# Sorting matrix of a block-sorted attention: two batches normalized on 128 partitions with column sums by TensorE, the other two later, and another load order

## The chip, the cores and the metric

The kernel runs on one core of one Trainium2 chip. The metric is the device time of one execution in microseconds (us); lower is better. The kernel before has three timed runs, with a median of 218.76 us (218.69 to 218.97). A further execution was profiled.

## The reference, cut to what matters

An attention over 4 batches, 8 heads, 768 positions and head size 64, whose keys and values are first mixed by blocks. P is an 8x8 matrix per head and batch, made from `sort_net` by five rounds of exp, row normalization and column normalization. The attention's output, 3072 tokens of width 512, goes through a feed-forward layer with a squared relu.

```
P = sort_net                                  # (4, 8, 8, 8)
for _ in range(5):
    P = exp(P - max(P, axis=-1))
    P = P / (sum(P, axis=-1) + 1e-09)
    P = P / (sum(P, axis=-2) + 1e-09)
k_sorted = einsum('bhij,bhjcd->bhicd', P, k_b)   # 8 blocks of 96 positions
v_sorted = einsum('bhij,bhjcd->bhicd', P, v_b)
attn = softmax(q_b @ k_sorted^T / 8)             # block by block, 96 x 96
x = (attn @ v_sorted) with heads side by side    # (3072, 512)
out = relu(x @ w_in) ** 2 @ w_out                # 512 -> 2048 -> 512
```

## The kernel before

Inputs are loaded by DMAs that POOL issues (function `dma`, line 319; the issue itself is L322) and that cast fp32 to bf16. Batch 0 is loaded as q in two halves of 64 partitions, then k and v by head pairs (k0, v0, k1, ... v3), then w_in in four quarters. w_out and batch 1 are loaded after the last of the three builds of w_all that POOL makes; batches 2 and 3 are loaded when attention of the batch before has come far enough (`load_late`).

P of all 32 heads lies on 32 partitions, 64 numbers each (`p_sb`). In each of five rounds ACT takes the exp (L432) and DVE normalizes rows, then columns (`sink_norm`, L400 to L402). Then DVE turns P (`p_turn`, L443), eight small matmuls spread it over the partitions (`p_spread`, L450), and `build_w` (L462) multiplies the spread P by a mask of the diagonal: w_all, the right side of the matmuls that mix k and v. For batch 0, w_all is built in pieces: heads 0 and 1, and 2 and 3, first half of the output blocks, by DVE; then, by POOL, heads 4 to 7 first half, heads 0 to 3 second half, heads 4 to 7 second half. The copy of the spread P, `pt` (L1075), is the source for all but the first. For batches 1 (second half of heads), 2 and 3, k and v are mixed by another form of P, `w_t` (`build_wt`, L487 and L494).

One unit of attention is a pair of heads. Its stages, with the letters that the order lists use, are K and V (`s_sort`, L588: mix k or v of the pair, then a copy), S (`s_sc`, L667 or L657: scores, then exp on ACT), T (`s_vt`, L723: transpose v, then a copy), A (`s_av`, L873: probabilities times v, then `norm` on DVE, L885 and L886) and X (`s_xt`, L928 or a DMA transpose: turn the result into xT). The first half of batch 0 (384 tokens) is computed first; its second half has K as `s_sort2` (L624). N is the mixing by w_t (`s_nat`, L759), Z the turning of k and q by DMA.

The feed-forward layer takes 384 tokens at a time: 64 "up" matmuls (L997), relu on ACT (L1005), square on DVE (L1008), 48 "down" matmuls (L1027), a copy and a DMA to the output. The first such unit needs xT of all four pairs of the first half of batch 0. Single matmuls of it, F0 to F7, are put ahead of that (`f_piece`, L955).

The order of the work on each engine is worked out before the program is written: every piece is an `Op` with an engine, a cost, and what it depends on, and `Plan.run` (L136) hands the pieces out in simulated time. On PE there are two lists, taken from the front only: attention and feed-forward. The attention piece goes if it could start earlier, or if its due number (a count of feed-forward pieces) is reached. On the other engines the piece that can start first goes; of equal ones, the one added first. Each engine then runs its pieces in that order. The string `FIRST` (L53) is the attention order of the first half of batch 0: a letter for the stage, a digit for the pair, a capital for a copy by ACT and a small letter for DVE, a quote mark for the other buffer in PSUM. `DUES` (L21) holds the due numbers of all later stages. Where PE would idle before its first feed-forward unit, `fill` (L418) puts matmuls on ones.

The softmax here doesn't subtract the row's maximum and nothing guards it: scores larger than these inputs give would overflow.

## Time and profile before

| What | Value |
|---|---|
| median of three runs | 218.76 us |
| the profiled execution | 218.47 us |
| its span, first to last instruction | 216.70 us |
| PE busy in the span | 210.8 us (97%) |
| first build of w_all begins | 11.88 us |
| last transposes of the first half of batch 0 begin | 20.90 us |
| last "down" matmul ends, by the chain of waits | 213.87 us |
| granted TensorE clock | 1.00 |

The profile is that of one execution. A row of the timeline gives start, busy time, engine, line, operation, what is written and read, and in brackets the idle time before it and what ended that. The chain of waits follows the work that ended last back from its end: each row is a start, a length and what was running. A busy PE is a PE with a matmul in it, filler matmuls included.

### The profile page before, as it was taken

The numbers are of one execution on the slowest core, as the hardware profiler recorded it, in microseconds if no ns is written. First come the engines' busy times: TensorE is split into PE (matmuls) and PEld (weight loads), VectorE is DVE, ScalarE is ACT, GpSimd is POOL, SyncE is SP. The second block draws the span as 40 slices with busy tenths as digits, with TensorE's granted clock in tenths as the row PEclk, the third lists the DMA queues.
The fourth block names the chain that finished last, engine by engine and source line by source line (L and its number), as shares of the span: only waits on it lengthen the run. The fifth ranks groups of instructions, "written<-read, shape, count | busy, mean of one in ns | idle before, by whom it ended". The sixth has DMA issues, their size and how long they took to land.

```text
span 216.7 us, 4912 instructions
## 1 busy us (share of the span) xinstructions
PE 210.8 (97%) x1942; PEld 120.1 (55%) x1958; DVE 109.9 (51%) x310; ACT 120.6 (56%) x246; POOL 30.5 (14%) x55
## 2 busy tenths in 40 slices
PE   8989999999999999999999999999999999999994
PEld 2566666446566565346675455446666465456543
DVE  6778748218784446506886055327676155005400
ACT  4665795237955277417884277238765276137521
POOL 7995223200000600000000420000000000000000
PEclk9999999999999999999999999999999999999999
DMA  5999999999983699299982599559996310120012
GB/s 66 196 202 207 207 207 206 184 222 274 201 176 98 123 192 215 51 182 205 242 158 78 125 193 213 109 142 127 257 188 135 91 51 0 48 82 18 0 48 97
DMA packets 47831, 31.51 MB, mean 145 GB/s; under 512 B 27264, under 2 KB 42880, under 8 KB 47808
## 3 DMA queue, kind: packets, MB, share of 16 engines
q0 software_dynamic: 12736, 13.63, 38.7%
q1 hardware_dynamic: 35072, 17.56, 36.5%
q8 instruction: 15, 0.25, 0.4%
q14 instruction: 8, 0.07, 0.1%
HBM read 29.70 MB, written 8.72 MB: 177 GB/s over the span
## 4 chain that ended last, share of the span: by engine, by line
PE 90%; DVE 5%; ACT 2%; issue 1%; DMA 1%; DVEq 0%
PE hp L997 38%; PE op L1027 36%; PE p L873 4%; PE p L657 3%; PE p L759 2%; PE op L1055 2%; PE p L667 1%; PE vbp L723 1%; DVE p_sb L402 1%; PE p L624 1%; DMA p_sb<-in_sort_net_dram 1%; ACT h L1005 1%; PE xtp L928 1%; DVE cs L400 1%; ACT p_sb L432 1%
## 5 line engine op out<-in xcount | busy, mean ns | idle before, releaser
L997 PE MATMUL hp<-xT,w_in_bf 128*128 128x384 bf16 x506 | 87.8, 326 | 0.0
L1027 PE MATMUL op<-w_out_bf,h 128*128 128x512 bf16 x352 | 83.5, 379 | 0.8
L1008 DVE TENSOR_TENSOR h<-h 128x384 bf16<-128x384 bf16 x128 | 43.9, 355 | 57.4 <-ACT h L1005 57.1
L1005 ACT ACTIVATE h<-hp 128x384 bf16<-128x384 f32 x128 | 62.0, 494 | 18.1 <-PE hp L997 15.6
L997 PEld LDWEIGHTS <-w_in_bf 128*128 128x128 bf16 x506 | 47.7, 98 | 31.3 <-issue 0.9
L1027 PEld LDWEIGHTS <-h 128*128 128x128 bf16 x368 | 34.4, 98 | 37.0 <-issue 1.0
L248 ACT COPY ob<-op 128x512 f32<-128x512 f32 (+2 forms) x25 | 14.2, 569 | 51.5 <-PE op L1027 49.1
L886 DVE TENSOR_TENSOR ao<-p,rec 96x512 bf16<-96x512 f32 x32 | 22.0, 687 | 1.1
L697 ACT ACTIVATE et<-p 96x384 bf16<-96x384 f32 x40 | 16.8, 486 | 8.0 <-PE p L657 7.7
L873 PEld LDWEIGHTS <-et 96*128 96x128 bf16 x256 | 11.6, 97 | 5.0 <-issue 0.7
L885 DVE RECIPROCAL rec<-p 96x8 f32<-96x8 f32 x32 | 6.4, 201 | 10.6 <-PE p L873 8.8
L1139 POOL COPY held<-xT 1x3 bf16<-1x3 bf16 (+1 forms) x2 | 0.4, 184 | 78.6 <-DMA xT<-ao 78.6
L418 PE MATMUL p<-ones 128*128 128x512 bf16 (+1 forms) x30 | 9.8, 449 | 1.1 <-DVE ones L269 1.1
L657 PEld LDWEIGHTS <-kx 128*128 128x128 bf16 x80 | 8.5, 144 | 2.3 <-issue 0.2
L873 PE MATMUL p<-vblk,et 96*128 96x65 bf16 x192 | 9.5, 193 | 0.0
L657 PE MATMUL p<-qz,kx 128*128 128x192 bf16 x80 | 9.0, 246 | 0.0
L250 DVE CAST kn<-p 128x768 bf16<-128x768 f32 x5 | 4.8, 957 | 8.3 <-PE p L759 8.1
L250 DVE CAST vn<-p 128x768 bf16<-128x768 f32 x6 | 5.7, 956 | 5.8 <-PE p L759 4.4
L322 POOL DMA_DIRECT2D kb<-in_k_dram x10 | 6.4, 637 | 4.4 <-DMA w_in_bf<-in_moe_w_in_dram 2.0
L322 POOL DMA_DIRECT2D qb<-in_q_dram x8 | 6.1, 769 | 5.8 <-DVE h L1008 3.3
L322 POOL DMA_DIRECT2D vb<-in_v_dram x10 | 6.2, 621 | 3.3 <-DMA w_in_bf<-in_moe_w_in_dram 3.3
L248 ACT CAST kn<-p 128x768 bf16<-128x768 f32 x5 | 4.0, 803 | 4.3 <-PE p L759 4.3
(84 smaller groups left out, 125.2 us busy)
## 6 DMA issues: line engine op xcount, KB each, us to landing
out_dram<-ob SPq DMA_DIRECT2D x23, 256.0 KB, 2.2
qb<-in_q_dram POOLq DMA_DIRECT2D x8, 384.0 KB, 11.3
v_way<-vn SPq DMA_DIRECT2D x6, 396.0 KB, 5.5
vblk<-v_way SPq DMA_DIRECT2D x6, 396.0 KB, 4.2
vb<-in_v_dram POOLq DMA_DIRECT2D x6, 384.0 KB, 12.0
kb<-in_k_dram POOLq DMA_DIRECT2D x6, 384.0 KB, 10.7
w_in_bf<-in_moe_w_in_dram POOLq DMA_DIRECT2D x4, 512.0 KB, 11.8
w_out_bf<-in_moe_w_out_dram POOLq DMA_DIRECT2D x4, 512.0 KB, 18.1
```

The lines of the kernel that those rows point to most:

```text
L248: nc.scalar.copy(out=out, in_=in_)
L250: nc.vector.tensor_copy(out=out, in_=in_)
L322: nc.gpsimd.dma_start(out=dst, in_=src)
L418: nc.tensor.matmul(out=p2[slot][:, 0, 0:128 * r].rearrange("p (r x) -> p r x", r=r), lhsT=ones, rhs=ones[:, None, :].to_broadcast([128, r, ...
L657: nc.tensor.matmul(out=scp[:, n // 2, 2 * BLK * (n % 2):2 * BLK * (n % 2 + 1)], lhsT=kx_r[u.kx][:, i::NB], rhs=qz_r[u.qz][:, :, :, C0 * i: ...
L697: nc.scalar.activation(out=et.rearrange("p h x -> p (h x)")[:, HS * h:HS * (h + 1)] .rearrange("p (m c a) -> p m c a", c=C0, a=NA), in_=st ...
L873: nc.tensor.matmul(out=oup[:, h, 66 * n:66 * n + D + 1], lhsT=(et_r[u.et[hf]].rearrange("p h x -> p (h x)") [:, BLK * (2 * n + h):BLK * (2 ...
L886: nc.vector.tensor_tensor(out=u.ao[:, n0:n0 + NQ, :, :].rearrange("p n e d -> p e n d"), in0=ov[:, :, :, 0:D], in1=rec[:, :, :, None].to_b ...
L997: nc.tensor.matmul(out=t["hp", nt][:, 0:HS], lhsT=w_in_bf[:, kc, 128 * nt:128 * (nt + 1)], rhs=xT[:, kc, t0:t0 + HS], start=(kc == 0), sto ...
L1005: nc.scalar.activation(out=t["h1", nt], in_=t["hp", nt][:, 0:HS], func=AF.Relu)
L1008: nc.vector.tensor_tensor(out=t["h2"][:, nt, :], in0=t["h1", nt], in1=t["h1", nt], op=ALU.mult)
L1027: nc.tensor.matmul(out=t["op", mt], lhsT=t["h2"][:, nt, 128 * mt:128 * (mt + 1)], rhs=w_out_bf[:, nt, :], start=(nt == 0), stop=(nt == NT ...
```

## The change

For batches 0 and 1, P lies on 128 partitions, one row of a matrix each (`pj`, 8 numbers). The exp gives the row sums as well (`accum_out`). Column sums are one fp32 matmul per round with a block-diagonal matrix of ones, `blk`, that DVE sets and POOL cuts out (`make_blk`). The last round writes P repeated 16 times, `pb`, and a single matmul with the identity spreads it. Fillers are planned ahead of the column-sum matmuls too.

P of batches 2 and 3 keeps the old form, and is made later (`late_p`), once the last pair of batch 0's second half is done; its `sel` is written by POOL and no longer by ACT. `build_wt` is called twice, for the second half of batch 1's heads and for batches 2 and 3.

Loads of batch 0 come in the order of `LOADS`; w_in comes in five pieces, the first two of two column tiles each (128 columns), and each "up" matmul waits for its own piece. The transposes of the second half of q move from ahead of P's spread into `FIRST` as Q0 to Q3, and those of the first half move in between the rounds of P. `FIRST` and `DUES` are new.

```diff
-FIRST = ("K0' v0 K1 v1 S0 t0 S1 t1' A0 k2' V2 A1 K3 S2 t2' v3 S3 x0 A2 T3' x1 A3 X2' F0 F3 F1 "
-         "x3 F4 F6 F7")
+LOADS = "q0 k0 v0 q1 k1 v1 k2 v2 k3 v3 w0"
+FIRST = ("P0 v0 Q3 k0 K1 S0 v1' T0' q2 S1 q1 K2' A0 V2 t1' S2 T2' A1 x0' K3 V3' A2 S3 t3 F0 x1' A3 "
+         "F3 x2 Q0 F1 x3 F4 F6 F7")
...
-    (2, "N"): (75.5, 70.5),
-    (2, "V"): (63.0, 88.5),
+    (2, "N"): (66.0, 82.5),
+    (2, "V"): (72.5, 88.5),
...
-    (3, "N"): (130.0, 137.5),
-    (3, "V"): (117.0, 140.5),
+    (3, "N"): (137.0, 139.0),
+    (3, "V"): (117.0, 142.0),
...
+    (2, "P"): (22.0,),
+    (2, "W"): (51.0,),
...
+    NF = 2 * H
+    pj = const.tile([128, NB], FP32)
+    nc.sync.dma_start(out=pj, in_=sort_net.rearrange("b h i j -> (b h i) j")[0:128, :])
     p_sb = const.tile([NH, NB, NB], FP32)
     nc.sync.dma_start(out=p_sb, in_=sort_net.rearrange("b h i j -> (b h) i j"))
...
+    blk = const.tile([128, 128], FP32)
+    nc.vector.memset(blk, 1.0)
...
     def load_w_in(g):
-        f = slice(d_ff // 4 * g, d_ff // 4 * (g + 1))
+        t0, t1 = ((0, 2), (2, 4), (4, 8), (8, 12), (12, 16))[g]
+        f = slice(128 * t0, 128 * t1)
...
-    load(0, 0, 0, H, slice(0, 64))
-    load(0, 0, 0, H, slice(64, 128))
-    id_op = plan.add("POOL", 0.4, lambda e: make_identity(nc, ident, nomemset=True))
+    def make_blk(e):
+
+        view = blk.rearrange("p (g x) -> p g x", x=NB)
+        for base, step, mult in ((0, -NB, 1), (NB - 1, NB, -1)):
+            nc.gpsimd.affine_select(
+                out=view, in_=view, compare_op=ALU.is_ge, fill=0.0, base=base,
+                pattern=[[step, 128 // NB], [0, NB]], channel_multiplier=mult)
+
+    load_next(1)
+    blk_op = plan.add("POOL", 0.65, make_blk)
+    id_op = plan.add("POOL", 0.35, lambda e: make_identity(nc, ident, nomemset=True))
+    load_next(4)
...
     plan.add("POOL", 1.5, make_mask, [id_op])
-    for g in range(HP):
-        load(0, 1, 2 * g, 2)
-        load(0, 2, 2 * g, 2)
-    load_w_in(0)
-    for g in range(1, 4):
+    load_next(len(loads))
+    for g in range(1, 5):
         load_w_in(g)
...
+    def by_rows(e):
+        nc.vector.reciprocal(out=rr, in_=rr)
+        nc.vector.tensor_tensor(out=pj, in0=pj, in1=rr.to_broadcast([128, NB]), op=ALU.mult)
+
+    def add_rows(e):
+        tiles["sums"] = ps1.tile([128, NB], FP32, tag="p1", name="sums")
+        nc.tensor.matmul(out=tiles["sums"], lhsT=blk, rhs=pj, start=True, stop=True)
+
+    def by_columns(e, last):
+        nc.vector.reciprocal(out=cr, in_=tiles["sums"])
+        if last:
+            nc.vector.tensor_tensor(
+                out=pb, in0=pj[:, :, None].to_broadcast([128, NB, C0]),
+                in1=cr[:, :, None].to_broadcast([128, NB, C0]), op=ALU.mult)
+        else:
+            nc.vector.tensor_tensor(out=pj, in0=pj, in1=cr, op=ALU.mult)
...
     for it in range(5):
-        step = plan.add("ACT", 0.26, lambda e: nc.scalar.activation(
-            out=p_sb, in_=p_sb, func=AF.Exp), [step])
+        step = plan.add("ACT", 0.25, lambda e: nc.scalar.activation(
+            out=pj, in_=pj, func=AF.Exp, accum_out=rr), [step])
         exps.append(step)
-        step = plan.add("DVE", 0.66, lambda e: sink_norm(e, 0), [step])
-        step = plan.add("DVE", 0.69, lambda e, it=it: sink_norm(e, 1, it == 4), [step])
+        step = plan.add("DVE", 0.36, by_rows, [step])
+        slot, old = r1.take()
+        step = plan.add("PE", 0.2, add_rows, [step, blk_op] + old)
+        fast.append(step)
+        r1.use(slot, step)
+        step = plan.add("DVE", 0.5 if it == 4 else 0.38, lambda e, it=it: by_columns(e, it == 4), [step])
+        r1.use(slot, step)
...
+    def late_p(due):
+
+        gate = x_done[0, HP - 1, 1]
+        picked = plan.add("POOL", 1.5, make_sel, [gate])
+        step = gate
+        for it in range(5):
+            step = plan.add("ACT", 0.26, lambda e: nc.scalar.activation(
+                out=p_sb, in_=p_sb, func=AF.Exp), [step])
+            for axis in range(2):
+                step = plan.add("DVE", 0.22, lambda e, axis=axis: late_sums(e, axis), [step])
+                step = plan.add("DVE", 0.2, lambda e, axis=axis: late_inverse(e, axis), [step])
+                step = plan.add("DVE", 0.22, lambda e, axis=axis, last=it == 4 and axis == 1:
+                                late_scale(e, axis, last), [step])
+        step = plan.add("DVE", 0.23, p_turn, [step])
...
+    def spread_first():
+        sf, old = rf.take()
+        pe = plan.add("PE", 0.1, p_spread, [last, id_op] + old)
+        spreads.append(pe)
+        w0 = build_w(0, 2, None, pe, 0, NQ)
+        cp = spread[0] = plan.add("ACT", 0.28, lambda e: nc.scalar.copy(out=pt, in_=tiles["pt_ps"]), [pe])
+        rf.use(sf, w0, cp)
+        build_w(2, 2, pt, cp, 0, NQ)
+        builds.extend(build_w(h0, 4, pt, cp, i0, NQ, "POOL") for h0, i0 in ((4, 0), (0, NQ), (4, NQ)))
...
+                if op in fast:
+                    fill(op.gap - 0.2, slot, 0.45 if op.begin < 4.5 else 0.24)
+                else:
+                    fill(op.gap - (0.5 if op in spreads else 0.05), slot)
```

## The prediction, made before the change was run

> **What bounds the kernel now.** I first read the page's shares and slices. PE is the engine to watch.
>
> ```profile
> PE 210.8 (97%) x1942; PEld 120.1 (55%) x1958; DVE 109.9 (51%) x310; ACT 120.6 (56%) x246; POOL 30.5 (14%) x55
> PE   8989999999999999999999999999999999999994
> DMA  5999999999983699299982599559996310120012
> ```
>
> A busy PE includes filler matmuls (the rows of L418), so I went on to the chain of waits, from 20 us.
>
> ```profile
> 20.15 0.70 DVE ao L886
> 20.85 0.05 issue
> 20.90 0.34 PE xtp L928 x4
> 21.24 0.49 PE hp L955 x3
> 21.73 0.88 PE p L624 x48
> 22.61 0.16 PE wtp L487 x4
> 22.77 1.73 PE hp L997 x10
> ...
> 85.87 0.50 ACT h L1005
> 86.37 0.02 issue
> 86.39 0.37 DVE h L1008
> ```
>
> From 20.90 us, the transposes that end head pair 3 of the first half (x3 in FIRST), the chain is PE work to 213.87 us, but for three places like the one at 85.87 (one each at 182.09 and 202.85) and some 0.05 us gaps. So there are two ways to change the time: move the 20.90, or add PE work behind it. What moves the 20.90? The timeline of POOL:
>
> ```profile
> 9.75 0.72 POOL L322 DMA_DIRECT2D vb<-in_v_dram  x1
> 10.46 2.30 POOL L322 DMA_DIRECT2D w_in_bf<-in_moe_w_in_dram  x3
> 12.98 0.74 POOL L322 DMA_DIRECT2D w_in_bf<-in_moe_w_in_dram  x1 [0.21 <-issue]
> 13.74 1.84 POOL L462 TENSOR_TENSOR w_all<-mask,pt 128x256 bf16<-128x256 bf16 x3
> 15.53 3.03 POOL L322 DMA_DIRECT2D w_out_bf<-in_moe_w_out_dram  x4
> 19.78 0.55 POOL L322 DMA_DIRECT2D vb<-in_v_dram  x1 [1.22 <-DMA w_in_bf<-in_moe_w_in_dram]
> ```
>
> POOL issues all loads of batch 0 and of w_in, and only then builds w_all for heads 4 to 7. The builds had their input since 12.57 us (pt cast, 12.20 + 0.37) and began at 13.74, when the last w_in load was issued. Issue-to-landing times of single loads give a second fact: v1, the 6th load, landed at 6.90 + 5.8 = 12.70 and the 14th was issued at 12.98; w_in 0, the 11th, landed at 10.46 + 9.0 = 19.46 and the 19th was issued at 19.78. An issue that waits begins some 0.3 us after the landing of the load eight before it.
>
> ```profile
> L322 POOL DMA_DIRECT2D kb<-in_k_dram x1: 716/716/716, 7.6 to 7.6; - x1
> DMA to landing us min/median/max: 6.8/6.8/6.8
> ```
>
> This is k2 (for heads 4 and 5), the 7th load: landed at 7.62 + 6.8 = 14.4. By the same sum v2 landed at 15.0, k3 at 16.0, v3 at 16.95.
>
> **What the Trainium skill says.** "TensorE: Matmul & The Clock Gate", section "Part 1: The HAM clock gate", gives about 427 ns per 512-column matmul on a cold array, about 216 warm. The trace agrees: fillers load their weights every 0.43 us up to 4.9 us; later 512-column matmuls take 0.216. The same page, section "Architectural detail", says that ScalarE, VectorE and GpSimd take their queues strictly in order, and that TensorE reorders nothing but weight loads; the POOL rows above agree (the builds wait 1.1 us behind loads). "FP8 and Floating Point Precision", section "TensorE Precision Notes", says a true fp32 product is four passes; no row of before shows one.
>
> **Part 1: the P chain.** Before, an iteration takes 4.07 - 2.31 = 1.76 us from exp to exp: one exp 0.26 and six DVE operations 0.21 + 0.19 + 0.21 + 0.25 + 0.19 + 0.21, with gaps. The first w_all build begins at 11.88. After, on 128 partitions: exp with row sums 0.25 (below: 0.19, fixed cost; above: 0.45 if the sum is a second instruction); two DVE operations 0.38; the fp32 matmul 0.35 (below 0.24, the wait from p_ij to the first spread matmul; above 0.6, four weight loads of 0.1 and the wait of one); reciprocal from PSUM and product 0.40; four changes of engine 0.2. That is 1.58, and 0.9 us less over five. The turn by DVE (0.23) and seven of eight spread matmuls go too: 0.9 and 0.5 for these turn 11.88 into about 10.5 (9.6 with all lower ends, 12.7 with all upper ones). One more cost is possible: fillers stand ahead of the sum matmuls on PE. The gap before the second is about 1.2 us and is filled at 0.24 each, with the array cold until about 5 us, so four of them take 1.7 and push the chain by 0.5, perhaps again in the third.
>
> **Part 2: what waits instead.** The new load order moves k0, v0 ahead of the second half of q; the bytes ahead of k2, v2, k3, v3 are the same and DMA is full from 4 us, so these land when they did. But POOL's list ahead of the builds grows by make_blk (two selects at the 0.32 of the ident row) and by one load, as w_in comes in five pieces. Sum: first load at 1.26, done 2.02; blk 2.7; ident 3.1; four loads at 0.72 to 6.0; mask 1.61 (3.84 to 5.45 before) to 7.6; six loads at 0.73 to 12.0; three pieces of w_in at 0.77 to 14.3. The 15th load needs the 7th, k2, landed: 14.4 + 0.3 = 14.7, issued by 15.45. First build 1.84 / 3 = 0.61: done at **16.1** (15.7 if nothing is limited to eight). Before it was 14.35, and K2 ran at 15.05 behind A0. P being ready 1.4 us earlier doesn't help: the planner gives POOL the loads first, as their start is never later than that of the builds.
>
> In the new FIRST, K2' stands before A0, V2, t1', S2, T2', A1, x0', K3. PE takes them in order, so all of these wait for 16.1, though A0 could run near 14.3 to 15 (before, it ran 14.69 - 11.88 = 2.8 after the first build; 10.5 + 2.8, and about 1 for the q and v1 pieces now ahead of it). From K2' on, with the durations of before: sort to copy 0.42, copy 0.48 on ACT; scores to exp 0.38, exp 0.80; transposes to copy 0.44, copy 0.42 on DVE or 0.58 on ACT; A to norm 0.5, norm 0.93. Times from K2': A0 0.2, t1' 0.76; norm 0 to 1.6 and the t1 copy behind it on DVE to 2.0, so A1 at 2.1; x0', K3 at 2.6, V3' at 2.8; ACT copies K3 to 3.5 and V3 to 4.0; S3 3.6, its exp to 4.8; t3 at 4.1, but its copy stands on DVE behind norm 1, x0 and norm 2, to 5.2; A3 5.3, norm to 6.65; x3 at 6.7. Before, it was 20.90 - 15.05 = 5.85 with A0, t1 and the q copies already out of the way. So x3 falls at 22.8; with 15.7 and DVE's order better than mine, 22.0. I take **22.5**, which is 1.6 later than 20.90 (1.1 to 2.0).
>
> **Part 3: late P.** Its spread is eight matmuls (0.26, the weight loads of that row before) and a second wtp group (0.16): 0.42 more PE work in the saturated part, up to 0.6 with changes of tiling. Its 30 DVE operations and five exps are 5 x 1.76 = 8.8 us from about 36 us on. DVE is busy 2.77 of 5 us from 35 to 40 and 2.63 of 10 from 40 to 50, so they fit; a square of L1008 may stand behind one waiting operation, and the down matmuls behind that square: 0 to 0.3, I take 0.1. If that cover were gone the price is one iteration, 1.8. sel moves to POOL, idle there from 39 to 71 us: nothing. The second p_sb load goes on SP behind the first, one issue of 0.40, with SP idle to 29 us: nothing.
>
> **Part 4: q and the due numbers.** Four groups of q transposes, hidden in the chain before, now stand in FIRST; three of them lie in PE's wait for K2', one in the norm of pair 3: nothing, 0.25 each on PE if that cover is gone. w0 with two tiles lands near 18.2 instead of 19.46, ahead of F0's turn: nothing. The due numbers reorder attention pieces of the same sizes; they can fill or lay open a stall like that at 85.87, of which 0.4 to 0.5 is real (two op matmuls run within the 0.9): -0.4 to +0.4, I take 0.
>
> **Sum.** 1.6 + 0.42 + 0.1 = +2.1 us. The profiled execution took 218.47 us (span 216.70 and 1.77 around it): 218.47 + 2.1 = **220.6**. The median of the runs is 218.76, 0.29 above the profiled one, so the forecast stands rather low against it.
>
> **Rivals.**
> A, builds not late (POOL gets to them before its last w_in issues, or faster): then v3's landing decides. 16.95 plus a bare chain (sort, copy, transpose, copy, A, norm: 3.5) puts x3 at 20.45, 0.45 earlier, and the 0.5 of part 3 takes it back: 218.5. For it: PE and ACT have room; against: the POOL rows. Chance 0.18.
> B, the gain comes through: P's 1.4 us earlier moves x3 by as much, 218.47 - 1.4 + 0.5 = 217.5; or A with the stalls filled, 218.1. One mechanism decides, whether anything stands between P and x3: it needs v3 well before 16.95 and the builds before 14. Against: the full DMA row, and 20.45 as the earliest x3. For: P's chain is all that PE waits for until 11.88. Chance 0.20, faster.
> C, worse: the cold fillers and four-pass matmuls put P at 12 to 12.7, the q pieces and S1 end after 16.1 and push A0 by 0.5 to 1; or late P holds the squares. 221.5. Chance 0.12.
> The forecast has 0.50.
>
> **How the numbers follow.** Against 218.76, a change of under 0.2% (0.44 us) is about what measurement can't tell from none: 218.3 to 219.2. Forecast and C are slower, 0.62; A is the same, 0.18; B is faster, 0.20. The range from 218.0 to 221.9 leaves out most of B and the worst of C. The likeliest case alone, slower, spans 219.7 to 221.3.
>
> **What would show it.** Right: POOL's w_all row begins near 15.5; PE waits on POOL for K2 at about 16; xtp of pair 3 begins after 22; the chain is solid PE from there, with a late-spread row and two wtp rows. Wrong: the sorts of heads 4 and 5 start by 14.6, or xtp begins before 21. Part 1 is wrong if the first w_all build is later than 11.6.

## The result, and the profile after the change

| | before | after |
|---|---|---|
| median of four runs | 218.87 us | 225.28 us (224.57 to 225.71) |
| ratio to before, 95% interval | | 1.0289 (1.0261 to 1.0318) |
| profiled execution / its span | 218.47 / 216.70 us | 225.71 / 224.0 us |
| first build of w_all begins | 11.88 | 12.35 |
| K2 begins on PE | 15.05 | 16.57 |
| last transposes of the first half begin | 20.90 | 24.50 |
| last down matmul ends | 213.87 | 220.77 |

The kernel became slower, by 6.4 us and not by the 2.1 of the forecast; 225.28 is above the range. In the profiled executions the difference is 225.71 - 218.47 = 7.24 us. It splits at the mark that the prediction used: 3.60 up to the last transposes of the first half, 3.30 from there to the last down matmul ((220.77 - 24.50) - (213.87 - 20.90)), and 0.40 - 0.06 in what lies behind and around the span.

Runs of one kernel that holds the change differ by up to 4.4 us, so most experiments below are read by places in their profiles (each a single run) rather than by their medians; a run over 1.5% above the fastest of its kernel counts as slow and is left out of medians and ratios, and as the profiles of e1 and e11 are of slow runs, only what comes before their last transposes of the first half is used.

The page's shares and slices of the kernel after:

```profile
PE 213.7 (95%) x1954; PEld 122.0 (54%) x1970; DVE 114.1 (51%) x334; ACT 120.0 (54%) x254; POOL 32.5 (15%) x59
...
PE   7987999997999999999999999999998999999994
...
DMA  5999999999598399759992679849996410111012
```

PE has 2.9 us more of busy time, but its share fell from 97% to 95%. The slices show two holes that before did not have: the 7 in the fourth (16.8 to 22.4 us) and the 7 in the tenth (50 to 56 us). The chain of waits names both (start, length, what ran):

```profile
17.89 1.20 issue
19.09 0.23 PE vbp L808
...
24.50 0.33 PE xtp L1013 x4
...
32.76 9.86 DMA xT<-ao
...
42.72 0.69 DVE ao L971
...
43.43 9.33 DMA xT<-ao
...
52.80 0.65 PE hp L1082 x3
53.45 0.28 PE late_ps L545 x8
```

The first hole is a pause of 1.20 us with no releaser (nothing that the profile shows ended it), in the middle of a group of four transposes. It has a section of its own below. The second is a chain by DMA: the first transpose of the second half of batch 0 takes 9.86 us, the last of the four norms (`ao`) waits on DVE for its buffer, the third transpose starts late and takes 9.33 us, and PE waits for it with unit 1, the second of the eight feed-forward units (they are counted from 0). The groups give that wait 1.42 us.

POOL, timeline of after:

```profile
2.25 0.89 POOL L383 TENSOR_SCALAR_AFFINE_SELECT blk<-blk 128x128 f32<-128x128 f32 x2
...
14.15 0.74 POOL L332 DMA_DIRECT2D w_in_bf<-in_moe_w_in_dram  x1 [0.24 <-DMA vb<-in_v_dram]
15.13 0.74 POOL L332 DMA_DIRECT2D w_in_bf<-in_moe_w_in_dram  x1 [0.24 <-DMA kb<-in_k_dram]
15.89 1.77 POOL L511 TENSOR_TENSOR w_all<-mask,pt 128x256 bf16<-128x256 bf16 x3
```

As the prediction said, POOL builds w_all behind its loads, the last of which wait for earlier loads to land; the builds begin at 15.89 (before: 13.74) and K2' on PE follows at 16.57.

The first round of the new P chain, timeline of after:

```profile
2.47 0.21 ACT L484 ACTIVATE pj<-pj 128x8 f32<-128x8 f32 x1 [0.37 <-DMA pj<-in_sort_net_dram]
2.59 0.18 ACT L484 ACTIVATION_READ_ACCUMULATOR pj<-pj 128x1 f32 x1
...
3.00 0.17 DVE L454 TENSOR_TENSOR pj<-pj,rr 128x8 f32<-128x8 f32 x1
3.31 0.57 PE L458 MATMUL sums<-pj,blk 128*128 128x8 f32 x2 [0.29 <-DVE pj L454]
...
3.92 0.21 DVE L461 RECIPROCAL cr<-sums 128x8 f32<-128x8 f32 x1 [0.75 <-PE sums L458]
4.16 0.17 DVE L467 TENSOR_TENSOR pj<-pj,cr 128x8 f32<-128x8 f32 x1
4.36 0.21 ACT L484 ACTIVATE pj<-pj 128x8 f32<-128x8 f32 x1 [1.59 <-DVE pj L467]
```

A round takes 4.36 - 2.47 = 1.89 us here, and 2.22, 2.03 and 1.63 after that. The row sum is a second instruction of ACT, and the column sum on a cold array takes 0.57 us as two matmuls. The P chain did not become faster at all: four rounds take 7.77 us, against 4 x 1.76 = 7.04 before.

### The profile page after: what moved, and what is told of

It is laid out like the page before. It is cut to its first block, busy times and chain, and to the rows that moved or that the text cites. A ratio compares the mean times of both kernels' runs of the same rounds, so it can differ in the third digit from the quotient of the medians.

```text
span 224.0 us, 4968 instructions
## 1 busy us (share of the span) xinstructions
PE 213.7 (95%) x1954; PEld 122.0 (54%) x1970; DVE 114.1 (51%) x334; ACT 120.0 (54%) x254; POOL 32.5 (15%) x59
## 3 DMA queue, kind: packets, MB, share of 16 engines
HBM read 29.71 MB, written 8.72 MB: 172 GB/s over the span
## 4 chain that ended last, share of the span: by engine, by line
PE 79%; DMA 9%; POOL 6%; issue 2%; ACT 1%; DVE 1%; POOLq 0%; DVEq 0%
PE hp L1082 34%; PE op L1112 30%; DMA xT<-ao 9%; PE p L958 4%; PE p L742 3%; POOL w_in_bf L332 2%; PE op L1140 2%; PE p L844 1%; POOL vb L332 1%; POOL kb L332 1%; PE p L752 1%; POOL qb L332 1%; ACT h L1090 1%; PE p L709 1%; PE vbp L808 1%
## 5 line engine op out<-in xcount | busy, mean ns | idle before, releaser
L1090 ACT ACTIVATE h<-hp 128x384 bf16<-128x384 f32 x128 | 61.3, 494 | 21.3 <-PE hp L1082 16.2
L1093 DVE TENSOR_TENSOR h<-h 128x384 bf16<-128x384 bf16 x128 | 44.5, 356 | 51.8 <-ACT h L1090 51.0
L253 ACT COPY ob<-op 128x512 f32<-128x512 f32 (+2 forms) x23 | 13.0, 566 | 48.4 <-PE op L1112 46.0
L958 PEld LDWEIGHTS <-et 96*128 96x128 bf16 x256 | 11.6, 97 | 5.7 <-issue 1.4
L255 DVE CAST kn<-p 128x768 bf16<-128x768 f32 x5 | 4.8, 958 | 14.4 <-PE p L844 14.3
L772 ACT ACTIVATE et<-p 96x768 bf16<-96x768 f32 x8 | 6.3, 806 | 1.6 <-PE p L752 1.5
```

The lines of the kernel that those rows point to most:

```text
L253: nc.scalar.copy(out=out, in_=in_)
L255: nc.vector.tensor_copy(out=out, in_=in_)
L958: nc.tensor.matmul(out=oup[:, h, 66 * n:66 * n + D + 1], lhsT=(et_r[u.et[hf]].rearrange("p h x -> p (h x)") [:, BLK * (2 * n + h):BLK * (2 ...
L1090: nc.scalar.activation(out=t["h1", nt], in_=t["hp", nt][:, 0:HS], func=AF.Relu)
L1093: nc.vector.tensor_tensor(out=t["h2"][:, nt, :], in0=t["h1", nt], in1=t["h1", nt], op=ALU.mult)
```

## The experiments

In all of them "last x" is the start of the last transposes of the first half, and "rest" is the time from there to the end of the last down matmul, all from PE's rows. An h marks a profile in which the array ran at half speed for some microseconds between 8 and 26 us, so that its last x is later than it would be; by its last x the clock is full again, so its rest can be used.

| kernel | median us | ratio to before (95%) | K2 | last x | rest |
|---|---|---|---|---|---|
| before | 218.87 | | 15.05 | 20.90 | 192.96 |
| after | 225.28 | 1.0289 (1.0261 to 1.0318) | 16.57 | 24.50 | 196.26 |
| e1_builds_first | 223.88 | 1.0225 (1.0129 to 1.0321) | 16.06 | - | - |
| e2_cold_fill | 227.47 | 1.0422 (1.0304 to 1.0540) | 18.12 | 26.85 h | 195.83 |
| e3_a0_first | 225.59 | 1.0309 (1.0263 to 1.0355) | 16.85 | 24.22 | 196.72 |
| e4_before_pool | 219.15 | 1.0025 (1.0012 to 1.0039) | 16.17 | 21.64 | 192.98 |
| e5_shift | 226.24 | 1.0324 (1.0281 to 1.0366) | 17.32 | 25.70 h | 196.05 |
| e6_ao4 | 223.49 | 1.0212 (1.0141 to 1.0283) | 17.28 | 25.08 h | 195.19 |
| e7_old_dues | 225.28 | 1.0268 (1.0208 to 1.0328) | 16.93 | 26.80 h | 194.06 |
| e8_late1 | 225.59 | 1.0269 (1.0205 to 1.0334) | 16.70 | 25.88 h | 195.76 |
| e9_before_builds | 218.67 | 0.9998 (0.9979 to 1.0016) | 15.27 | 21.12 | 192.97 |
| e10_q_late | 223.16 | 1.0188 (1.0155 to 1.0222) | 15.16 | 23.65 | 195.80 |
| e11_p_q_late | 223.87 | 1.0239 (1.0189 to 1.0288) | 15.04 | - | - |
| e12_blk_first | 223.13 | 1.0190 (1.0161 to 1.0220) | 15.21 | 23.85 | 195.64 |
| e13_split | 226.83 | 1.0357 (1.0292 to 1.0422) | 19.78 | 27.49 h | 194.00 |
| e14_p_alone | 223.29 | 1.0220 (1.0161 to 1.0279) | 16.52 | 22.68 | 194.43 |
| e15_p_alone_ao4 | 223.56 | 1.0225 (1.0189 to 1.0261) | 17.19 | 23.73 | 194.94 |
| e16_q_last | 226.59 | 1.0363 (1.0325 to 1.0401) | 14.90 | 22.15 | 198.81 |
| e17_dues_ao4 | 224.46 | 1.0258 (1.0186 to 1.0330) | 17.39 | 24.45 | 194.13 |
| e18_p_alone_512 | 222.43 | 1.0168 (1.0117 to 1.0220) | 16.51 | 22.35 | 194.60 |

### What makes the first half late

**e1_builds_first**, the kernel after with four w_in loads handed to POOL after the builds:

```diff
     load_next(len(loads))
-    for g in range(1, 5):
-        load_w_in(g)
...
         builds.extend(build_w(h0, 4, pt, cp, i0, NQ, "POOL") for h0, i0 in ((4, 0), (0, NQ), (4, NQ)))
+        for g in range(1, 5):
+            load_w_in(g)
```

> The changed kernel, but w_in pieces 1 to 4 are handed to POOL after its three builds of w_all. Theory (builds late behind loads): the first POOL build begins near 13 instead of 15.89, the sort of head pair 2 near 14.5 to 15 instead of 16.57, the last transposes of the first half near 22.3 instead of 24.50, and the time falls by 2 to 3.5 us (the wait for the DMA transposes at 52.8 shrinks with it) to 222 to 223.3. Rival (P itself is late by its fillers, 12.35): the sorts stay bound by P, time falls by under 0.7. Rival (due numbers and late P): no change.

The builds began at 13.80, but K2' only at 16.06, 0.5 earlier than in after: S0 (14.26), v1', S1 (15.48) and q1 (15.76) stand ahead of it in FIRST and came late themselves. So two limits lie 0.5 us apart, and the lateness of POOL was worth 0.5 of the 1.5. The pause of 1.20 stays. In time, 223.88 (222.13 to 224.67) lies between theory and rivals.

**e4_before_pool** asks the reverse: the kernel before, with make_blk on POOL (unused) and w_in in five pieces.

```diff
+    plan.add("POOL", 0.65, make_blk)
     id_op = plan.add("POOL", 0.4, lambda e: make_identity(nc, ident, nomemset=True))
...
-    for g in range(1, 4):
+    for g in range(1, 5):
         load_w_in(g)
```

> The kernel before, with POOL's list made as long as the changed kernel's: make_blk (its result is not used) and w_in in five pieces. Theory (builds late): POOL's first build begins near 15.3 instead of 13.74, the sort of pair 2 near 16 instead of 15.05; slower by 1 to 2 us, 219.9 to 220.9. Rivals (P chain, late P, due numbers): no change within 0.3.

```profile
16.17 0.38 PE L603 MATMUL tp<-w_all,kb 128*64 128x64 bf16 x12 [0.49 <-POOL w_all L477]
```

K2 now waits for POOL, 1.12 later than in before, and 0.74 of that reaches the last transposes (21.64); the rest is untouched. The mechanism of the prediction's second part exists, at about 0.5 us of time, less than the 1 to 2 us of the theory.

**e9_before_builds** takes POOL's lateness out of the kernel before:

```diff
     load_w_in(0)
-    for g in range(1, 4):
-        load_w_in(g)
...
+    for g in range(1, 4):
+        load_w_in(g, builds[-1:])
     loads_after(builds[-1:])
```

> The kernel before, with the last three w_in loads issued by POOL after the three builds of w_all instead of before them. Theory 1 (in the kernel before, the builds by POOL were not the last to arrive: K2 stood behind A0 on PE and k3 and v3 landed at 16.0 and 16.95): builds begin near 12.6 instead of 13.74, the last transposes of the first half stay within 0.2 of 20.90, time 218.8 +- 0.2. Rival (POOL's lateness already set the end of the first half in the kernel before): they come up to 1.1 us earlier, time 217.8 to 218.3.

The builds began at 12.87 and the last transposes at 21.12; no change in time. In the kernel before, the builds were not the last to arrive.

**e3_a0_first**, another order in FIRST:

```diff
-S1 q1 K2' A0 V2 t1' S2 T2' A1 x0' K3 V3'
+S1 q1 t1' A0 K2' V2 A1 S2 T2' K3 x0' V3'
```

> The changed kernel, but in FIRST t1' and A0 stand ahead of K2', and A1 and K3 one place earlier. Theory (work queued behind K2' on PE): K2' stays near 16.5, but the last transposes come 1 to 1.5 us earlier (near 23.2), time falls by 1 to 2.5, to 223 to 224.3. Rival (the DMA transposes of the second half set the time by themselves): under 0.5.

The last transposes moved by 0.28 only, and the pause is there again (1.14, until 18.55). As long as it stands, A0 behind K2' is not what costs.

**e2_cold_fill**: fillers ahead of the column sums are counted at 0.45 us each up to 7.0 us instead of 4.5, so there are fewer.

```diff
-fill(op.gap - 0.2, slot, 0.45 if op.begin < 4.5 else 0.24)
+fill(op.gap - 0.2, slot, 0.45 if op.begin < 7.0 else 0.24)
```

> The changed kernel, but fillers ahead of the column-sum matmuls are counted at 0.45 us each until 7.0 us instead of 4.5. Theory (builds late): the first build of w_all by DVE moves from 12.35 to about 11.3, but the sort of pair 2 stays at 16.5; the time falls by 0 to 0.5, to 224.8 to 225.3. Rival (P late by fillers): the last transposes move by 1 and the time falls by 1 to 1.5.

The spread came 0.25 earlier (11.76), but the array was at half speed until 25 us:

```profile
PEclk9755799999999999999999999999999999999999
```

The fillers delay the sums, as the prediction feared. That they can't be spared is likely, not shown: two of the four runs had a clock of 0.992 and 1.00, and were as slow (229.66 and 227.28).

**e12_blk_first** and its base **e11_p_q_late** (the kernel after with the old due numbers, w_in pieces behind the builds, q's second half loaded behind v3 and turned late in FIRST); e12 puts `make_blk` ahead of the first load.

```diff
-    load_next(1)
     blk_op = plan.add("POOL", 0.65, make_blk)
...
-    load_next(4)
+    load_next(5)
```

> The kernel after with everything of the run before: its order of loads and of first-half stages, its due numbers, w_in pieces behind the builds. What is left of the change is the new P chain, late P, make_blk and the five w_in pieces. Theory 1 (the new P chain ends 0.5 us later than the old one, and late P costs 1.1 us in the dense part; the rest of the 6.4 us came from orders and due numbers): 1.6 us above the run before, about 219.5, and up to 1.2 more if PE's stall in its instruction stream falls on busy time. Rival (the P chain is what cost the time): about 3 us or more above the run before. Other rival (the P chain pays off once nothing else is late): level with the run before or under it.

> As the run before, with blk made by POOL ahead of its first load instead of behind it (the first load starts 0.9 later). Theory 1 (the first sum waited 1.16 us for blk, and every later round starts from there): first sum at about 2.5 instead of 3.3, first build of w_all at about 11.6 instead of 12.35, time 0.7 less than the run before. Rival (the filler matmuls ahead of the sums, 0.43 us each on a cold array, set the rounds): first build at 12.2 or later, time the same within 0.2.

In e12 the second exp began at 4.35 (after: 4.36), and the first build at 12.14 (11.97 in e11): theory 1 was wrong. The first build fits the rival's 12.2 nearly; the time can't tell, as e11's runs spread from 222.84 to 226.00. The weight load's wait of 1.16 us for blk in after was no loss, since pj was ready no earlier (3.00 + 0.17). e11 came 0.7 over its base e10 (below) and e12 level with it, within what runs of one kernel differ by, so this pair does not size the P chain's cost. All three have the pause that comes next.

### The pause of PE

**e5_shift**: the first four fillers become sixteen of a quarter of the size.

```diff
+    def fill_small(n):
+        for _ in range(n):
+            nc.tensor.matmul(out=p2[0][:, 0, 0:128], lhsT=ones, rhs=ones, start=True, stop=True)
...
-    plan.add("PE", 1.6, lambda e: fill(0.96, 0), ...)
+    plan.add("PE", 1.6, lambda e: fill_small(16), ...)
```

> The first four filler matmuls (128x512) become sixteen of 128x128: twelve more matmuls and weight loads ahead of everything, with about the same work. In the kernel after and two variants, PE stood still for 1.14 to 1.20 us before its 223rd matmul, whichever operation that was. Theory 1 (the stall belongs to a place in PE's instruction stream): it comes again before about the 223rd matmul, which is now twelve matmuls earlier in the order of work, in the mixing of V2 or the A0 matmuls; time 225 +- 0.7. Theory 2 (the stall belongs to the operation or to a wait that the trace does not show): it stays in the transposes of v of pair 1. Theory 3 (it belongs to a moment or to chance): it is gone or elsewhere, and the time falls by up to 1.2 us to about 224.

Matmuls were counted through the timelines. After, before its 223rd:

```profile
17.55 0.34 PE L808 MATMUL vbp<-ident,kvT 128*128 128x128 bf16 x3
19.09 0.23 PE L808 MATMUL vbp<-ident,kvT 128*128 128x128 bf16 x1 [1.20 <-issue]
```

e5, before its 223rd, which is another operation:

```profile
17.99 0.25 PE L677 MATMUL tp<-w_all,vb 128*64 128x64 bf16 x3
19.07 0.34 PE L677 MATMUL tp<-w_all,vb 128*64 128x64 bf16 x9 [0.83 <-issue]
```

So the pause belongs to a place in PE's stream (in e3, e11 and e12, too, a matmul of V2 stands there). It is not a mark of the new P: e10 below, with the old one, has one of 1.14 before its 224th matmul, and e9, which differs from e10 only in when the second half of q is loaded and turned, has none.

**e13_split** moves some 60 more matmuls ahead of that place (every filler of 512 columns as four of 128); **e18_p_alone_512** and **e14_p_alone** put the new P chain, late P, make_blk and the five w_in pieces into the load order, first-half order and due numbers of before, with builds ahead of the w_in loads; e14 with split fillers, e18 without.

```diff
-LOADS = "q0 k0 v0 q1 k1 v1 k2 v2 k3 v3 w0"
+LOADS = "q0 q1 k0 v0 k1 v1 k2 v2 k3 v3 w0"
...
+FIRST = ("Q0 Q1 P0 K0' v0 Q2 K1 v1 Q3 S0 t0 S1 t1' A0 k2' V2 A1 K3 ...
...
-        for r in [4] * n + [2] * (us - one * n > one / 2):
+        for r in [1] * (4 * n + 2 * (us - one * n > one / 2)):
```

> The kernel after with every filler of 128x512 as four of 128x128 (16 of those took the same 1.89 us as four of 128x512): some 60 more matmuls early, so the 223rd matmul is one that runs at about 15.5 us instead of 17.9. Theory 1 (the pause falls on a place in PE's stream only if that place is reached between about 17.4 and 18.3, since the kernels that reach it at 15.3 to 16.4, or after 19, show none): no pause, last transposes 1.2 earlier at 23.3, clock 1.00, time 225.3 - 1.2 = 224.1 or less. Rival (place alone): the pause comes before the 223rd matmul, at about 15.5, and K2' waits for POOL until 16.6 anyway; the time falls by up to 1 us too, but the pause is seen.

> The new P chain, make_blk, late P and the five w_in pieces, with the rest as before: load order, order of the first half's stages (q's second half around P), due numbers, builds by POOL before its w_in loads; fillers split, so without the pause. Theory 1 (P chain +0.5 at the first build, last transposes at about 21.4; late P +1.1 behind that): 218.8 + 1.6 = 220.4. Rival (late P or the P chain is the larger cost): 222 or more. Other rival (P's new form pays): 218.8 or less.

> The new P chain, make_blk, late P and five w_in pieces in the order and due numbers of before, fillers of 128x512 as in after. Theory 1 (PE pauses at the ends of blocks of 256 instructions, 128 matmuls with their weight loads, when it gets there before something that comes late): a pause before the 223rd matmul, reached at about 17; last transposes at 22.7 + 0.5 to 1.2; time about 223.5. Rival (the pause has to do with the orders of after): no pause, last transposes at 22.7 or earlier, about 222.

e13, e14 and e18 reached the 223rd matmul at some 18.6, 14.3 and 16.8 us, with no pause there: for e18 the rival was right, and e13 had no pause, as its theory said, but no gain either, as its array did not warm up until 23 us. In time e14's rival was nearer (223.29, where 222 or more was given), and e18 met its own (222.43). But e14 has a pause elsewhere:

```profile
19.05 0.30 PE L750 MATMUL p<-qT,kvT 64*128 64x96 bf16 x5
19.51 0.24 PE L750 MATMUL p<-qT,kvT 64*128 64x96 bf16 x3 [0.16 <-issue]
```

This is before its 351st matmul, and so is the pause of 0.54 in e15: 128 matmuls further on, which with their weight loads are 256 instructions. What PE needs at such a place can be found in the DMA records of the traces. The page of after (queue, kind: packets, MB, share):

```profile
q8 instruction: 15, 0.25, 0.4%
```

These 15 packets have 16 KB each, one for every 262 of the 3924 matmuls and weight loads. When they came, and when PE reached the two places, in us:

| kernel, matmul | PE could start it | packet ends | it starts | behind the packet |
|---|---|---|---|---|
| before, 223rd | 15.26 | 13.32 | 15.26 | 1.94 |
| e18, 223rd | 16.81 | 15.51 | 16.81 | 1.30 |
| after, 223rd | 17.89 | 17.77 | 19.09 | 1.32 |
| e10, 224th | 17.40 | 17.04 | 18.54 | 1.50 |
| e8, 223rd | 18.02 | 18.31 | 19.61 | 1.30 |
| e14, 351st | 19.35 | 18.17 | 19.51 | 1.34 |
| e15, 351st | 20.02 | 19.12 | 20.56 | 1.44 |

The first packet goes with the 223rd matmul, the second with the 351st (in e10 the 224th and 352nd). In all 20 profiles neither matmul starts less than 1.29 us behind the end of its packet. PE stands still at twelve of these places (at the first in after, e1, e3, e5, e7, e8, e10, e11, e12 and e17, at the second in e14 and e15), and these twelve matmuls start 1.29 to 1.62 us behind it. So by all times on record the pause is a wait for PE's own next instructions. No run moved a packet and nothing else, so no edit shows it.

The packet starts 1.5 to 4.3 us after PE has come to the place 128 matmuls earlier, so the pace of PE from there on decides. In before, the 95th matmul stands in the P chain, at 9.24, and PE takes 6.02 us to the 223rd. In after, 36 of the 48 small matmuls that turn q's second half have moved behind P's spread, and the others behind the 223rd matmul; so the 95th falls in the dense stretch, at 13.10, and PE is at the 223rd 4.79 us later. The packet began 3.73 us and ended 4.67 us behind the 95th, and the 1.32 come on top.

Six profiles with a pause or a wait of 0.8 to 1.6 us near that place (e1, e5, e6, e7, e8, e11) show the granted clock at 0.50 from 18.1 to 20.6 us on, for 3.4 us (e7 and e11: 6.8); after, e3, e10, e12 and e17 don't. The same kernel has both (e17: clock 1.00 in two runs of 222.92 and 223.56 us, 0.992 in two of 225.35 and 225.55). A part of the spread of the runs comes from there; not all, as e14's runs, all at a clock of 1.00 or 0.999, spread from 222.06 to 224.94.

### What is lost behind the first half

**e6_ao4**: four buffers for ao (pb moves into a free part of xT).

```diff
-    rqT, rao, rks, rvs, ret = Ring(4), Ring(3), Ring(3), Ring(3), Ring(4)
+    rqT, rao, rks, rvs, ret = Ring(4), Ring(4), Ring(3), Ring(3), Ring(4)
...
-                    u.ao = att.tile([96, u.ni, 2, D], BF16, tag="ao", name="ao", bufs=3)
+                    u.ao = att.tile([96, u.ni, 2, D], BF16, tag="ao", name="ao", bufs=4)
```

> Four buffers instead of three for the attention result ao (pb moves into a free part of xT to make room). Theory 1 (the third norm of batch 0's second half waited 1.17 us on DVE for the first DMA transpose to hand back its buffer, so the third transpose was issued late and the second feed-forward unit waited 1.42 us): the third transpose is issued 1 us or more earlier, PE's wait of 1.42 us shrinks below 0.4, time 225.3 - 1.2 = 224.1. Rival (the transposes are slow because DMA is full of loads, 9 to 10 us each, and an earlier issue only lengthens them): they land when they did, the wait stays near 1.4, time 225.3.

Chain of waits of e6, where after has the two DMA rows:

```profile
46.53 5.29 PE op L1112 x24
51.82 0.65 PE hp L1082 x4
```

No wait is left: the last ao was written at 40.66 instead of 42.72. Unit 2 starts 55.30 us behind the last transposes, against 56.86 in after and 54.60 in before: 1.56 back, of which 1.1 survives to the end; the other part goes in a wait in unit 5, of the kind shown below. The transposes were as slow (9.81, 7.20 and 9.67 us), and the third was issued earlier: theory 1 holds for this kernel.

**e7_old_dues**: the kernel after with the due numbers of before, those of late P and its w_t kept.

```diff
-    (0, "K"): (-132.5, -45.5, -116.0, -71.5),
+    (0, "K"): (-133.5, -48.0, -102.0, -78.0),
...
-    (3, "X"): (157.5, 238.0, 172.5, 328.0),
+    (3, "X"): (159.0, 248.0, 167.0, 326.0),
     (2, "P"): (22.0,),
     (2, "W"): (51.0,),
```

> The kernel after with the due numbers of before (only those of late P and of its w_t are kept). Theory 1 (the due numbers were set for other times, but cost or gain under 0.4 us): 225.3 +- 0.5, and last transposes of the first half at 24.5 as in after. Rival (the new due numbers put the second half of batch 0 too late, and cause the wait of 1.42 us for its DMA transposes and later ones): the transposes are issued up to 3.6 us earlier, as before, and the time falls by 1.4 or more, to 223.9 or less.

The rest falls from 196.26 to 194.06, 2.2 us, more than the rival's 1.4, and no wait for DMA transposes is left. But it is not the rival's way: the first transpose was issued 8.24 us behind the last transposes of the first half, and in after 8.26. The profiled time does not show the gain, because the pause and half speed took it back before the mark.

**e17_dues_ao4** has both edits.

> The kernel after with the due numbers of before and four ao buffers. Theory 1 (3.3 us are lost behind the last transposes of the first half: 1.5 by the wait for DMA transposes, 0.7 by the new due numbers, 1.1 by late P's own work): from the last transposes to the end of the last down matmul 194.0 +- 0.3 us instead of 196.26 (before: 192.96); with the last transposes at 24.5 the time is 223.2. Rival (late P's work holds norms and squares whatever the orders): 195.5 or more.

The rest is 194.13, as expected; 1.17 over before stays. But the shares that theory 1 gives to buffers and due numbers are not shown: e7 has the old three buffers, and e13 has the due numbers and the buffers of after, differs from it in the split of the fillers alone, and comes to 194.00. Unit 2 begins 55.49 us behind the last transposes in e17 and 55.28 in e13, against 56.86 in after; units 2 to 5 take 96.91 and 96.99 us, against 97.67 (before: 96.64). The chain of waits of e13, where after has its DMA rows:

```profile
48.92 5.29 PE op L1112 x24
54.21 0.65 PE hp L1082 x4
```

Its third transpose took 6.34 us instead of 9.33, and PE did not wait. In unit 5, after has a second wait, and e13 none:

```profile
169.38 0.41 PE L958 MATMUL p<-vblk,et 96*128 96x65 bf16 x8 [0.52 <-ACT et L782]
```

```profile
170.11 0.41 PE L958 MATMUL p<-vblk,et 96*128 96x65 bf16 x8
```

Here too it is a transfer that comes last: `vblk<-v_way` was issued at 163.36 in after and took 5.89 us, until 169.25; in e13 it took 4.34. This wait is not the due numbers': e10, with the old P and the old numbers, has it (0.90), and e5, with the new ones, does not. Without the two waits, units 2 to 5 take 96.99 and 97.00 us with the new numbers (e13, e5) and 96.91 to 97.20 with the old (e7, e12, e14, e15, e17, e18, all with late P), so the due numbers as such cost nothing that shows. Four kernels with late P have neither wait (e7, e13, e14, e17); their rest is 194.00 to 194.43, which leaves 1.0 to 1.5 us for late P. What makes a transfer slow in one of these kernels and not in the other stays open.

**e8_late1**: late P with one round of five (it leaves out four, so the kernel computes something else).

```diff
         step = gate
-        for it in range(5):
+        for it in range(4, 5):
```

> Late P makes one of its five rounds (the other four are left out, so P of batches 2 and 3 is another one); 24 DVE operations and 4 exps fewer. Theory 1 (late P lies beside PE's work and costs only its 0.4 us of PE, which stay here): 225.3, by no more than 0.3 less. Rival (late P's DVE and ACT operations hold the norms, squares and exps of this stretch): the ao buffer's wait and PE's wait of 1.42 us shrink, time 224.3 or less.

The rest is 0.5 less than in after: between the theories. PE's wait for the transposes is 0.69 instead of 1.42 us (unit 1 begins at 53.74 behind a transpose of 9.00 us), that for `vblk` 0.85 instead of 0.52. As e13 loses both with all five rounds in place, the difference can't be put down to late P's operations.

### The P chain by itself, and other orders

e18 (above) is the cleanest: 222.43 us, 3.7 over before, of which 1.45 lies before the mark and 1.64 behind it. It has no pause, and its P is as early as the old one (first build at 11.92, before 11.88), yet the last transposes come at 22.35. The chain goes back to v1, which runs at 14.19 instead of 13.13 (and to a group of q's transposes behind it). Its load, in e18:

```profile
L332 POOL DMA_DIRECT2D vb<-in_v_dram x1: 733/733/733, 7.7 to 7.7; - x1
...
DMA to landing us min/median/max: 6.3/6.3/6.3
```

7.74 + 6.3 = 14.0, where before had 6.90 + 5.8 = 12.7. POOL issues v1 0.84 later, because make_blk (0.89) stands ahead of the loads, and then DMA is short of work. The windows of before and after, whose last column is GB/s:

```profile
6.00:8.00 2.00, 1.00 1.31 203
8.00:10.00 2.00, 1.00 1.31 191
```

```profile
6.00:8.00 2.00, 1.00 1.16 160
8.00:10.00 2.00, 1.00 1.25 182
```

From 4 to 12 us, after moved 1432 KB against 1568 in before (from the windows of 2 us), 136 KB or 0.7 us less. In e18 the window from 6 to 8 us has 129 GB/s.

**e15_p_alone_ao4** is e14 with four ao buffers.

> As the run before with four ao buffers. Theory 1 (the third buffer is waited for only when the first DMA transpose starts after 31 us, as in after; here it starts at about 29.7): same as the run before within 0.3. Rival (late P's DVE work delays the norms whatever the buffers): same too, but with a wait of PE for the DMA transposes in both.

No gain (223.56 and 223.29 us). A fourth buffer helps only where the third transpose is held up by it, as in after.

**e10_q_late** (the kernel before; builds before w_in loads; q's second half loaded behind v3, its transposes late in FIRST) and **e16_q_last** (q's second half behind w_in's first piece, its transposes after x3; K2, V2, K3, V3 earlier in FIRST; split fillers) tried for a kernel that beats both.

```diff
-    load(0, 0, 0, H, slice(64, 128))
     id_op = plan.add("POOL", 0.4, ...)
...
+    load(0, 0, 0, H, slice(64, 128))
     load_w_in(0)
...
-FIRST = ("K0' v0 K1 v1 S0 t0 S1 t1' A0 k2' V2 A1 K3 S2 t2' v3 S3 x0 A2 T3' x1 A3 X2' F0 F3 F1 "
-         "x3 F4 F6 F7")
+FIRST = "K0' v0 K1 v1 S0 t0 S1 t1' A0 k2' V2 A1 K3 S2 t2' v3 S3 x0 A2 T3' x1 A3 Q0 X2' Q1 Q2 Q3 F0 F3 F1 x3 F4 F6 F7"
```

> As the run before, and the load of the second half of q (64 partitions, not needed by the first 384 tokens) stands behind v3 instead of ahead of k0; its transposes stand late in FIRST. Theory 1 (DMA's order bounds the first half: v3 landed at 16.95 and k3 at 16.0, each held by the 0.8 MB of q's second half): k3 and v3 land 3 us or more earlier, K3 and V3 no longer wait, the last transposes come at about 20.0, time 217.9. Rival (ACT, DVE and PE need that time anyway, or w_in decides): the loads land earlier but the last transposes stay at 20.9, time 218.8; or the second half waits for its q, over 219.

> The kernel before with builds before the w_in loads, q's second half loaded behind w_in's first piece and turned after x3, K2, V2, K3, V3 ahead in FIRST, fillers split. Theory 1 (with loads and builds early, the chain from P on is bound by PE, ACT and DVE, and the pause is gone): last transposes at 20.0, time 217.9. Rival (the order of first-half stages is bound by the copies and exps of ACT and DVE, so the early loads are worth nothing): 20.9 or later, 218.8 or more.

Both failed. In e10 K2 and K3 ran at 15.16 and 16.02, as in before (15.05 and 16.04; they stand behind A0), the pause of 1.14 came in, w_in's first piece came later, and the last transposes fell at 23.65. Then, with the old P and the old due numbers, unit 1 waited for DMA transposes of 9.30 and 9.74 us as in after: rest 195.80, 2.8 over before. In e16 the late transposes of q held unit 0 until 25.6. None of the runs beat the kernel before; e9 equals it.

## Why the prediction was wrong, point by point

**The mark at 20.90** as the place to read the change from was right, and so was the sign. The forecast moved it by 1.6 us and what lies behind it by 0.5; they moved by 3.60 and 3.30.

**Part 1, the P chain** (1.58 per round, first build at 10.5): wrong for all rounds but the last, which took 1.63 on a warm array. The row sum is a second instruction, with which an exp takes 0.30 us (2.47 to 2.77), between the 0.25 and the upper end of 0.45. The column sum came as two matmuls with two weight loads, where the upper end had four weight loads; it takes 0.57 cold and 0.39 warm. Fillers of 0.42 stand ahead of the second and third sum, as the working feared. Rounds of 1.63 to 2.22 put the first build at 12.35, beyond the 11.6 that the prediction named. By itself this cost little: with the build at 11.92 in e18 the first half ended late all the same.

**Part 2, POOL's builds** (done at 16.1, last transposes computed at 22.8, taken as 22.5): the mechanism was right. 24.50 is 2.0 later than the forecast, term by term: 0.3 was shaved off the sum without a row to support it; K2' ran at 16.57 and not 16.1; from K2' to the last transposes it took 7.93, which is the 1.20 of the pause and 6.73, where the sum had 6.7. The 0.47 goes back to a step that failed: **"the bytes ahead of k2, v2, k3, v3 are the same and DMA is full from 4 us, so these land when they did"**. DMA was not full while POOL was busy with make_blk and the mask, and k2, at 8.49 + 6.4, landed at 14.9 instead of 14.4; v3, at 10.62 + 8.4, at 19.0 instead of 16.95, and w0 at 20.2 instead of 18.2, still ahead of F0. And the builds alone were not the whole lateness (e1: 0.5 of 1.5 us): the order of FIRST and the late loads were as late.

**Part 4, the transposes of q** ("hidden in the chain before, now stand in FIRST [...] nothing, 0.25 each on PE if that cover is gone"): this is the step that failed worst ahead of the mark. It counted their work, and not that PE's whole stream shifts: the place where PE needs its next block of instructions came into the dense stretch, and PE stood still there for 1.20 us. No row of before shows such a pause, so it could not be read from there.

**Behind the mark**, the prediction took it that everything shifts with the mark, but for late P: no step asked what a shift does to the transfers there. This is the largest part of the error, 2.26 of the 3.30 us. By comparison with e13, which has neither wait, 1.58 go with the wait for the DMA transposes and 0.68 with that for `vblk`. In before the first transpose was issued at 29.18 and took 7.4 us; e18: 30.60 and 7.95; e14: 30.93 and 8.72; e10: 31.93 and 9.30; after: 32.76 and 9.86. e10 shows that a shift of 2.75 is enough for both waits, whatever P does. That the loads of batch 1 slow the transposes is likely, but was not tried alone.

**Part 3, late P** (0.42 of PE and 0.1): PE's share was right: 0.28 for the spread and 0.12 more for the two w_t groups. But with the two waits gone 1.0 to 1.5 are left (e7, e13, e14, e17), so 0.6 to 1.1 are not told by those rows, and e8 does not tell them either. The remainder stays open.

**Part 4, the due numbers** (0, at most 0.4 either way): right as far as the runs show. Units 2 to 5 take as long with the new numbers as with the old once the wait for `vblk` is gone (e5, e13), and the 0.68 and 0.76 that e7 and e17 gain there are that wait for the most part. The stall at 85.87 did go, as it could, but other waits came.

**The sum** in the profiles: K2' 1.52, the pause 1.20, the chain behind it 0.88; what goes with the transposes' wait 1.58, with that for `vblk` 0.68, late P and what goes with it 1.04; 0.34 at the end. Together 7.24. The terms ahead of the mark are stages one behind the other, not what each would give back: e10 and e12 have K2 at 15.2, as before, and the pause makes them late all the same (23.65 and 23.85). The rivals: A fell with the builds at 15.89, B with the first build at 12.35; C named cold fillers, slow sums and late P and pointed the right way, but not to the pause or the two transfers, which are 3.5 of the 7.2 us.

## What to carry to other kernels

When a change shifts the start of a saturated stretch, follow the transfers in it as well: ask for each what it will now overlap with and which buffer it hands back, since a shift of some 3 us cost 2.3 to 2.8 more here (after, e10), and less in kernels whose transfers happened to be faster (e7, e13). Instructions are such a transfer, too: PE got its own in blocks of 256, and small matmuls that left the quiet start for the dense stretch cost 1.2 us, not because of their work, but because PE then came to the end of a block before the next one was there. An instruction that is put ahead of loads on the queue that issues them costs twice, in the issue and in the gap of the DMA behind it; a full DMA row holds only as long as the queue keeps it full. And a short dependent chain of tiny operations gained nothing from more partitions here: four rounds on 128 partitions with one column-sum step on PE took 7.77 us, with six DVE operations on 32 partitions 7.04.

## What the runs showed of the hardware that was not expected

- PE stood still for 0.16 to 1.59 us without a releaser before its 223rd (or 224th) and its 351st matmul, 128 matmuls with their weight loads apart. It went on 1.29 to 1.62 us behind the end of a 16 KB packet of instructions, which had started 1.5 to 4.3 us after PE came to the place 128 matmuls earlier (20 profiles).
- Near such a pause, or a wait as long, the granted clock was often 0.50 for 3.4 or 6.8 us. The Trainium skill, "TensorE: Matmul & The Clock Gate", section "Part 1: The HAM clock gate", gives a window of 3.4 us that runs freely. The traces agree: stretches of one clock early in the profiles last 3.41, 6.83, 10.24, 13.65 and 17.07 us (e2, e6, e7, e11), and e17 has runs with the fall and without. The same section gives half speed after a window of idleness; here the clock fell around pauses and waits of 0.8 to 1.6 us in six profiles, and not in five, so less than a whole window of idleness can come with it.
- The first 52 fillers are the same in e13 and e14; the array was warm from 23.3 us in the one and from 6.7 us in the other.
- Sixteen fillers of 128 columns took as long as four of 512: 1.89 us (e5, after).
- DMA transposes of the same size took 7.4 us in one place and 9 to 10 us when issued 3 us later.
